# A token mixer in the frequency domain and a feed-forward layer in one kernel: uniform frequency slots, 96-row constants, part of batch 1 in the prologue, and a wider slot plan

## The chip, the cores and the metric

The kernel runs on one core of a Trainium2 chip. Its time is the device time of one execution in microseconds (us), as the median of several runs; smaller is better. The core's engines are TensorE (PE; its weight loads are shown as PEld), VectorE (DVE), ScalarE (ACT), GpSimd (POOL) and SyncE (SP, which only issues transfers here). Each works through its own instructions in the order in which they were written, and waits for the others by semaphores. POOL issues the transfers that change float32 into float16 on the way; SP issues plain ones.

## What is computed

```python
def _attn_ref(x, filt_r, filt_i):            # x: 8 batches x 3008 tokens x 256 channels
    X = np.fft.rfft(x, axis=1)
    F = (filt_r + 1j * filt_i)[None, :, :]   # 1505 frequencies x 256 channels
    return np.fft.irfft(X * F, n=x.shape[1], axis=1).astype(np.float32)

def _moe_ref(x, w_in, w_out):                # x: 24064 tokens x 256, d_ff = 2048
    h = x @ w_in
    g = np.maximum(0.01 * h, h)
    return (g @ w_out).astype(np.float32)
```

The first function mixes the 3008 tokens of a batch, channel by channel, by a filter on their Fourier transform; the second is applied to every token of the result. All inputs and the output are float32; the kernel computes in float16 with float32 sums.

## The kernel before

**The transform in two steps.** 3008 is 94 x 32, so the transform over the tokens is one over 94 (n1) and one over 32 (n2). For each batch the kernel runs this chain of stages:

- *s1* (16 groups, `s1_group`): two matmuls with the constants `f1_sb` (94 rows), 256 columns each, into one PSUM tile. ACT copies the tile to a buffer `big` as float16 (`spread`, L224).
- *t1* (4 parts, `t1_part`): DVE transposes blocks of 32 x 32 from one `big` buffer to the next (`turn`, L230).
- *s2* (12 groups, `s2_group`): one matmul with `small_sb` (L248; two in group 0, L246), then three products with the filter's real part `fa_sb` and imaginary part `fb_sb` on DVE (L252, L253, L254) and one sum on POOL (L256). Batch 0 uses another form, `s2_wide`: four columns at a time, two products on DVE (L272, L273), no POOL.
- *sa* (12 groups, `sa_group`, L284): the inverse over n2, copied to a third `big` buffer by ACT through `spread` (L224).
- *t2* (4 parts): transposes as in t1.
- *sb* (16 groups, `sb_group`, L300): four small matmuls with the constants `i1_sb`, copied by DVE (in batch 0 by DVE and ACT in turn) to `yts[b % 2]`, the batch's mixed tokens with the channels on the partitions (L303).

**The feed-forward layer in slots.** The 24064 tokens are cut into 47 chunks of 512. A chunk takes eight slots of `moe1_group` (4 matmuls of 512 columns, L322, then the leaky ReLU on ACT, L327) and, one chunk later, eight slots of `moe2_slice` (8 matmuls of 256 columns, L335; every fourth slot ACT copies the sum out, L339, and SP stores it). So there are 376 slots, and eight at the end with the second product alone. The chunks of one batch are 47 slots long.

**What sets the order.** The order is written by hand, with no scheduler. Batch 0 runs all its stages before slot 0; this is the prologue. The stages of batch b from 1 on are handed to slots by `plan`, with a base of 0 for batch 1 and 47(b-1)-8 for the others, to be done when the chunks reach that batch. Within a slot PE gets `moe1_group`, then the stages' groups in the order in which `plan` put them there, then `moe2_slice`. As PE works in order, a group that waits holds up the second product of its own slot and all that follows.

**The buffers that tie the stages together.** s1, s2, sa and sb take their PSUM tiles from one pool, `pfp`, of two tiles, in turn: a group waits until the tile's last reader, two groups before, is done with it. `moe1_group` and `s2_wide` use the pool `php` (two tiles), `moe2_slice` the pool `pop` (two tiles). `x_sb` holds one batch's input, so the load of the next waits for the last s1 matmul. The three `big` buffers rotate from stage to stage.

**Special cases of the frequency layout.** The 94-point step keeps 47 frequencies k1 and packs the special one at 0 and that at 47 into one place. So group 0 of s2 and sa uses other matrices (`fwd2(1)`, `inv2(1)`), the filter needs extra one-row loads (L183, L200), memsets (L191, L192, L204, L205), and a copy and a sign change of the filter to the upper 64 partitions, which `filt_copy` makes on DVE (L186, L187). L206 clears a whole `big` buffer on DVE.

**Loads in the prologue.** SP issues `f1_sb` in two halves of 94 rows, `small_sb` and `i1_sb`. POOL issues x of batch 0 in eight pieces (L162), the filter in pieces of 16 rows (L176, L180, L183), `w_in`, `w_out`, and x of batch 1. From the ninth on, each of POOL's transfers waits for the one eight before it to land.

Of the kernel before, what the change touches and what calls it, by code (L numbers as in the profile page):

```python
# [22 lines left out]

def _build_np_constants(N):
    n1 = np.arange(N1)
    c = np.arange(NC)
    fwd1 = np.zeros((P, N2, P))
    inv1 = np.zeros((P, N2, N1))
    for n2 in range(N2):
        for s, (qr, qi) in enumerate(((0, 2), (1, 3))):  # L30
            k1 = c + NC * s
            ang = 2 * np.pi * (np.outer(n1, k1) / N1 + n2 * k1[None, :] / N)
            co, si = np.cos(ang), np.sin(ang)
            ire, iim = 2 * co, -2 * si
            re, im = co, -si
            if s == 0:
                alt = np.cos(np.pi * n1)
                re[:, 0], im[:, 0] = 1.0, alt
                ire[:, 0], iim[:, 0] = 1.0, alt
            else:  # L40
                for m in (re, im, ire, iim):
                    m[:, NC - 1] = 0.0
            fwd1[:N1, n2, qr * Q : qr * Q + NC] = re
            fwd1[:N1, n2, qi * Q : qi * Q + NC] = im
            inv1[qr * Q : qr * Q + NC, n2, :] = ire.T / N1
            inv1[qi * Q : qi * Q + NC, n2, :] = iim.T / N1
# [8 lines left out]
    r_0, i_0, r_47, i_47 = (np.zeros((N2, N2)) for _ in range(4))
    r_0[:, 0] = 1.0
    i_0[:, 0] = np.cos(np.pi * n2)
    j = np.arange(1, h)
    r_0[:, 1:h] = np.cos(2 * np.pi * np.outer(n2, j) / N2)
    i_0[:, 1:h] = -np.sin(2 * np.pi * np.outer(n2, j) / N2)  # L60
    j = np.arange(h)
    r_47[:, h:] = np.cos(2 * np.pi * np.outer(n2, 1 + 2 * j) / (2 * N2))
    i_47[:, h:] = -np.sin(2 * np.pi * np.outer(n2, 1 + 2 * j) / (2 * N2))


    sg = np.where(k2 < h, 1.0, -1.0)[None, :]
# [4 lines left out]
    fwd2 = np.zeros((P, 2, P))
    inv2 = np.zeros((P, 2, P))
    for sp in range(2):
        f, g = np.zeros((P, P)), np.zeros((P, P))
        for s in range(2):
            if sp and s == 0:
                blk(f, 0, 0, r_0), blk(f, 0, 2, i_0)
                blk(f, 2, 0, r_47), blk(f, 2, 2, i_47)
                w0 = np.full((N2, 1), 2.0)
                w0[0] = 1.0  # L80
                blk(g, 0, 0, w0 * r_0.T), blk(g, 2, 0, w0 * i_0.T)
                blk(g, 0, 2, 2 * r_47.T), blk(g, 2, 2, 2 * i_47.T)
                continue
            blk(f, s, s, co), blk(f, s + 2, s, si)
            blk(f, s, s + 2, -si * sg), blk(f, s + 2, s + 2, co * sg)
            blk(g, s, s, co.T), blk(g, s + 2, s, -(si * sg).T)
            blk(g, s, s + 2, si.T), blk(g, s + 2, s + 2, (co * sg).T)
        fwd2[:, sp, :] = f
        inv2[:, sp, :] = g / N2
# [8 lines left out]
def kernel(  # L98
# [35 lines left out]
    fny_sb = cpool.tile([1, D], FP16, name="fny_sb")  # L134
# [13 lines left out]
    def fwd2(sp):  # L148
        return small_sb[:, sp, :]

    def inv2(sp):
        return small_sb[:, 2 + sp, :]

    def inv2x(sp):
        return small_sb[:, 4 + sp, :]
# [16 lines left out]
    def filt_load(dst, src, c0, c1):  # L172
        h = N2 // 2
        for s in range(2):
            q = s * Q
            nc.gpsimd.dma_start(  # L176
                dst[q : q + h, c0:c1], rows(src, NC * s + c0, N1, 1, h, c1 - c0))

            lo, hi = max(c0, 1 - s), min(c1, NC - s)
            nc.gpsimd.dma_start(  # L180
                dst[q + h : q + Q, lo:hi], rows(src, N1 - NC * s - lo, N1, -1, h, hi - lo))
        if c0 == 0:
            nc.gpsimd.dma_start(dst[h:Q, 0:1], rows(src, N1 // 2, N1, 1, h, 1))  # L183

    def filt_copy(c0, c1):
# [1 line left out]
        nc.vector.tensor_scalar(out=fb_sb[64:P, c0:c1, :], in0=fb_sb[0:64, c0:c1, :],  # L187
                                scalar1=-1.0, scalar2=None, op0=AL.mult)
# [17 lines left out]
    nc.vector.memset(big[2][:], 0.0)  # L206
# [4 lines left out]
    def s1_group(b, g):  # L211
        def go():
            ps = pfp.tile([P, 2, D], FP32, tag="pf", name=f"s1_b{b}_g{g}")
            for j in range(2):
# [1 line left out]
                nc.tensor.matmul(ps[:, j, :], f1_sb[:, n2, :], x_sb[:N1, n2, :],  # L216
                                 start=True, stop=True)
            spread(big[(4 * b) % 3], g, ps)
# [3 lines left out]
    def spread(dst, g, ps):  # L222
        o = dst[:].rearrange("p (e n t) -> p e n t", n=Q, t=2)[:, :, ds(2 * g, 2), :]
        nc.scalar.copy(o, ps[:].rearrange("p n (e t) -> p e n t", t=2))  # L224

    def turn(src, dst, i, parts):
        w = D // 2 // parts
# [2 lines left out]
        nc.vector.transpose(o, a)  # L230
# [195 lines left out]
```

## Time and profile before

| | us |
|---|---|
| time, median of 3 runs (859.57 to 862.3) | 860.71 |
| the profiled execution's own time | 862.13 |
| its span, from the first to the last instruction | 860.4 |
| first matmul of the feed-forward layer starts at | 88.12 |
| PE busy, share of the span | 775.4, 90% |
| ACT busy | 547.6, 64% |
| DVE busy | 372.5, 43% |
| POOL busy | 130.4, 15% |

In the profile the numbers of tiles are left out, so `f1_sb` reads f_sb, `i1_sb` reads i_sb, the PSUM tiles of s1 and of s2 both read s_b_g (s_b_w for the wide form), those of sb sb_b_g and those of sa sa_b_g. A row of the timeline has the start, the length, the engine, the line, the operation, what is written and read, how many instructions were merged, and in brackets the engine's idle time before it with what ended that. A line number tells the stage, but L216 is every s1 matmul and L224 every copy by `spread`, whatever the batch.

### The profile page before, as it was taken

Reading aid. Unit: us, or ns where it says so; the run is one execution under the profiler, and the core shown is the slowest. Engines: PE = TensorE matmul, PEld = TensorE weight load, DVE = VectorE, ACT = ScalarE, POOL = GpSimd, SP = SyncE. Lnnn points to the kernel's source line nnn. Section 1 sums busy time; section 2 is a strip of 40 time slices with the busy share of each in tenths; the row PEclk is TensorE's granted clock in tenths of the full one; section 3 lists DMA queues with packets and bytes.
Section 4 is the critical chain, followed back from the end, with each engine's and each line's share of the span. In section 5 each row is a group of like instructions: output and inputs, shape, how many; then the busy total and the mean of one; then the engine's idle time right before and its main releaser. Section 6 shows DMA issues by size and latency. Waiting matters only on the chain.

```text
span 860.4 us, 13332 instructions
## 1 busy us (share of the span) xinstructions
PE 775.4 (90%) x5725; PEld 528.4 (61%) x5725; DVE 372.5 (43%) x458; ACT 547.6 (64%) x704; POOL 130.4 (15%) x131
## 2 busy tenths in 40 slices
PE   0334879999999999999999999999999999999998
PEld 0112445776567756776567856776577756776666
DVE  0197176607742377307651476307651476300000
ACT  1313846686666866586666866586667766566663
POOL 4300024002400042002400042002400042000000
PEclk9996899999999999999999999999999999999999
DMA  7670030004011410114110401114011101011111
GB/s 153 105 136 1 13 85 25 29 34 109 26 38 37 98 37 25 38 40 94 38 37 26 110 25 37 37 38 97 26 37 38 37 26 37 26 37 46 41 38 50
DMA packets 31803, 43.21 MB, mean 50 GB/s; under 512 B 2266, under 2 KB 30010, under 8 KB 31086
## 3 DMA queue, kind: packets, MB, share of 16 engines
q0 software_dynamic: 5696, 15.98, 10.4%
q1 hardware_dynamic: 26048, 26.38, 8.8%
q8 instruction: 45, 0.74, 0.4%
q14 instruction: 14, 0.11, 0.0%
HBM read 33.69 MB, written 24.64 MB: 68 GB/s over the span
## 4 chain that ended last, share of the span: by engine, by line
PE 72%; DVE 19%; DMA 4%; issue 2%; ACT 2%; POOL 1%; DVEq 0%; ACTq 0%; POOLq 0%
PE o_c_t L335 32%; PE h_c_g L322 31%; DVE p_b_g L253 5%; DVE p_b_g L252 5%; DVE p_b_g L254 4%; PE sb_b_g L300 3%; PE s_b_g L216 3%; DVE big L230 2%; PE s_b_g L248 2%; DMA fb_sb<-in_filt_i_dram 2%; DMA x_sb<-in_x_dram 2%; PE sa_b_g L284 1%; ACT big L224 1%; ACT gt_c L327 1%; DVE y_b_g L273 1%
## 5 line engine op out<-in xcount | busy, mean ns | idle before, releaser
L327 ACT ACTIVATE gt_c<-h_c_g 128x1024 f16<-128x1024 f32 x376 | 386.4, 1028 | 223.1 <-PE h_c_g L322 223.0
L335 PE MATMUL o_c_t<-w_out_sb,gt_c 128*128 128x256 f16 x3008 | 389.3, 273 | 0.0
L322 PE MATMUL h_c_g<-yt,w_in_sb 128*128 128x512 f16 (+7 forms) x1728 | 388.9, 353 | 0.3 <-DVE yt L303 0.3
L335 PEld LDWEIGHTS <-gt_c 128*128 128x128 f16 x3008 | 290.8, 98 | 107.3 <-issue 27.3
L322 PEld LDWEIGHTS <-w_in_sb 128*128 128x128 f16 x1728 | 163.5, 98 | 95.5 <-issue 2.1
L230 DVE STREAM_TRANSPOSE big<-big 128x1024 f32<-128x1024 f32 x64 | 116.2, 1929 | 192.2 <-ACT big L224 192.1
L256 POOL TENSOR_TENSOR y_b_g<-p_b_g,p_b_g 128x512 f16<-128x512 f32 x84 | 106.7, 1270 | 245.2 <-DVE p_b_g L254 242.4
L303 DVE CAST yt<-sb_b_g 128x376 f16<-128x376 f32 x120 | 60.7, 545 | 79.9 <-PE sb_b_g L300 79.9
L224 ACT CAST big<-s_b_g 128x512 f16<-128x512 f32 x128 | 69.9, 614 | 27.1 <-PE s_b_g L216 27.1
L252 DVE TENSOR_TENSOR p_b_g<-s_b_g,fa_sb 128x512 f32<-128x512 f32 x84 | 58.1, 692 | 60.0 <-PE s_b_g L248 47.5
L224 ACT CAST big<-sa_b_g 128x512 f16<-128x512 f32 x96 | 55.5, 581 | 27.6 <-PE sa_b_g L284 27.6
L216 PE MATMUL s_b_g<-x_sb,f_sb 94*128 94x256 f16 x256 | 44.1, 291 | 30.3 <-DMA f_sb<-fwd_const 27.4
L339 ACT COPY ost_c_t<-o_c_t 128x512 f32<-128x512 f32 x94 | 55.5, 591 | 18.3 <-PE o_c_t L335 13.7
L162 POOL DMA_DIRECT2D x_sb<-in_x_dram x22 | 11.8, 542 | 320.7 <-PE s_b_g L216 319.6
L253 DVE TENSOR_TENSOR p_b_g<-s_b_g,fb_sb 64x512 f32<-64x512 f32 x84 | 58.2, 693 | 1.1
L254 DVE TENSOR_TENSOR p_b_g<-s_b_g,fb_sb 64x512 f32<-64x512 f32 x84 | 57.4, 684 | 1.1
L216 PEld LDWEIGHTS <-f_sb 94*128 94x128 f16 x256 | 25.2, 102 | 46.4 <-DMA f_sb<-fwd_const 27.9
L300 PEld LDWEIGHTS <-big 128*128 128x128 f16 x512 | 30.8, 104 | 24.9 <-DVE big L230 8.6
L284 PE MATMUL sa_b_g<-y_b_g,small_sb 128*128 128x512 f16 (+1 forms) x117 | 41.4, 388 | 4.2 <-DVE y_b_g L273 2.7
L248 PE MATMUL s_b_g<-big,small_sb 128*128 128x512 f16 x77 | 29.1, 378 | 17.1 <-DVE p_b_g L254 15.7
L300 PE MATMUL sb_b_g<-i_sb,big 128*128 128x94 f16 x512 | 35.3, 215 | 9.9 <-DVE big L230 7.6
L284 PEld LDWEIGHTS <-small_sb 128*128 128x128 f16 x117 | 11.5, 102 | 21.4 <-issue 5.9
(33 smaller groups left out, 60.4 us busy)
## 6 DMA issues: line engine op xcount, KB each, us to landing
out_dram<-ost_c_t SPq DMA_DIRECT2D x94, 256.0 KB, 2.1
x_sb<-in_x_dram POOLq DMA_DIRECT2D x7, 1024.0 KB, 8.6
x_sb<-in_x_dram POOLq DMA_DIRECT2D x7, 480.0 KB, 10.5
x_sb<-in_x_dram POOLq DMA_DIRECT2D x4, 256.0 KB, 11.9
w_in_sb<-in_moe_w_in_dram POOLq DMA_DIRECT2D x1, 1024.0 KB, 8.4
w_out_sb<-in_moe_w_out_dram POOLq DMA_DIRECT2D x1, 1024.0 KB, 13.0
f_sb<-fwd_const SPq DMA_DIRECT2D x2, 376.0 KB
i_sb<-inv_const SPq DMA_DIRECT2D x1, 752.0 KB, 34.3
```

The costliest lines, as they stand in the source:

```text
L216: nc.tensor.matmul(ps[:, j, :], f1_sb[:, n2, :], x_sb[:N1, n2, :], start=True, stop=True)
L224: nc.scalar.copy(o, ps[:].rearrange("p n (e t) -> p e n t", t=2))
L230: nc.vector.transpose(o, a)
L252: nc.vector.tensor_tensor(p1[:], ps[:], fa, AL.mult)
L253: nc.vector.tensor_tensor(p2[0:64], ps[64:P], fb[64:P], AL.mult)
L254: nc.vector.tensor_tensor(p2[64:P], ps[0:64], fb[0:64], AL.mult)
L256: nc.gpsimd.tensor_tensor(y1[:], p1[:], p2[:], AL.add)
L284: nc.tensor.matmul(ps[:, ds(*js), :], m(sp), t[:, ds(*js), :], start=(i == 0), stop=(i == len(y) - 1))
L300: nc.tensor.matmul(ps[:, j, :], src[:, n2, ts(dt, P)], i1_sb[:, n2, :], start=True, stop=True)
L322: nc.tensor.matmul(ph[:, j, ds(o, ln)], w_in_sb[:, dt, ts(ct, P)], yts[b % 2][:, dt, ds(lo, ln)], start=(dt == 0), stop=(dt == NDT - 1),)
L327: nc.scalar.activation(gts[ci][:, ds(2 * g, 2), :], ph[:], AF.Lrelu)
L335: nc.tensor.matmul(po[:, tj % 2, :], gts[ci][:, ct, ts(tj, P)], w_out_sb[:, ct, :], start=(ct == 0), stop=(ct == NCT - 1))
```

## The change

- **Uniform slots for k1.** Frequencies 0 and 47 now have places of their own: 48 places, none special. Group 0 of s2 and sa has one form like the others, `small_sb` shrinks from 6 to 3 matrices, and the one-row loads, the small memsets and `fny_sb` are gone. The clearing of `big[2]` covers columns 24 to 31 alone and no longer stands behind anything on DVE.
- **Constants.** `f1_sb` has 96 rows (two are zeros; matmuls read 94) and comes in four parts. SP issues it and `small_sb` first. `i1_sb` is issued by ACT after the copies of s1.
- **The filter's upper half** is written by ACT (fa, L317 of the changed kernel) and by POOL (fb, L318) in place of DVE.
- **The prologue.** s1 of batch 0 takes tiles from two pools and is copied by ACT and DVE in turn. s1 of batch 1 is run between the sb groups of batch 0, with tiles from `pop` and copies by ACT. `sb_group` counts the lower 128 channels first, then the upper.
- **The slot plan.** For batches 2 to 7, with z = 47(b-1)-8: s1 in slots z-5 to z+2 (before z to z+7), t1 from z+4 (z+9), s2 from z+9 with 7 slots for 4 groups (z+13, 5 for 4), sa three slots after s2, t2 from z+34 (z+32), sb in z+39 to z+46 (z+36 to z+43). For batch 1: no s1, t1 from slot 0 (8), s2 from slot 4 with 6 slots for 4 groups (slot 11, one a slot), t2 from 26 (27), sb from 31 (30).

```diff
-    f1_sb = cpool.tile([N1, N2, P], FP16, name="f1_sb")
+    f1_sb = cpool.tile([R1, N2, P], FP16, name="f1_sb")      # R1 = 96
-    nc.sync.dma_start(f1_sb[:, 0:H2, :], f1_d.ap()[0])
+    for i in range(FP):                                      # FP = 4
+        nc.sync.dma_start(f1_sb[:, ts(i, step), :], f1_d.ap()[i])
+    nc.sync.dma_start(small_sb[:], small_d.ap())
     x_load(0, 4)
-    nc.sync.dma_start(f1_sb[:, H2:N2, :], f1_d.ap()[1])
-    nc.sync.dma_start(small_sb[:], small_d.ap())
-    nc.gpsimd.dma_start(fny_sb[:], filt_r[N // 2 : N // 2 + 1, :])
...
-    nc.vector.memset(big[2][:], 0.0)
     nc.gpsimd.dma_start(w_in_sb[:], moe_w_in.rearrange("(dt p) c -> p dt c", p=P))
-    nc.gpsimd.dma_start(w_out_sb[:], moe_w_out.rearrange("(ct p) d -> p ct d", p=P))
+    nc.vector.memset(big[2][:].rearrange("p (e n t) -> p e n t", n=Q, t=2)[:, :, NC:Q, :], 0.0)
...
-            spread(big[(4 * b) % 3], g, ps)
+            spread(big[(4 * b) % 3], g, ps, copy)
...
-            if g == 0:
-                for j in range(2):
-                    nc.tensor.matmul(ps[:, j, :], fwd2(1 - j), src[:, j, :], start=True, stop=True)
-            else:
-                nc.tensor.matmul(ps[:], fwd2(0), src[:, ds(2 * g, 2), :], start=True, stop=True)
+            s2_mm(b, 2 * g, ps[:])
...
-    def plan(b, base, t1, s2, t2, sb, step):
+    def plan(b, s1, t1, s2, step, lag, t2, sb):
         for g in range(16):
-            at(base + g // 2, s1_group(b, g))
+            if s1 is not None:
+                at(s1 + g // 2, s1_group(b, g))
+            at(sb + g // 2, sb_group(b, g, nc.vector.tensor_copy))
         if b + 1 < B:
-            at(base + 8, lambda: x_load(b + 1, 1))
+            at(0 if s1 is None else s1 + 8, lambda: x_load(b + 1, 1))
         for i in range(4):
-            at(base + t1 + i // 2, t1_part(b, i))
-            at(base + t2 + i // 2, t2_part(b, i))
+            at(t1 + i, t1_part(b, i))
+            at(t2 + i, t2_part(b, i))
         for g in range(12):
-            at(base + s2 + (step * g) // 4, s2_group(b, g))
-            at(base + s2 + 3 + (step * g) // 4, sa_group(b, g))
-        for g in range(16):
-            at(base + sb + g // 2, sb_group(b, g, nc.vector.tensor_copy))
+            at(s2 + (step * g) // 4, s2_group(b, g))
+            at(s2 + lag + (step * g) // 4, sa_group(b, g))
+    two = ((pfp, "pf"), (php, "ph"))
+    copies = (nc.scalar.copy, nc.vector.tensor_copy)
     for g in range(16):
-        s1_group(0, g)()
+        s1_group(0, g, two[(g // 2) % 2], copies[g % 2])()
+    nc.scalar.dma_start(i1_sb[:], i1_d.ap())
+    for c0 in (0, HC):
+        nc.scalar.copy(fa_sb[64:P, c0 : c0 + HC, :], fa_sb[0:64, c0 : c0 + HC, :])
+        nc.gpsimd.tensor_scalar(fb_sb[64:P, c0 : c0 + HC, :], fb_sb[0:64, c0 : c0 + HC, :],
+                                -1.0, None, AL.mult)
     x_load(1, 1)
-    filt_copy(0, HC)
+    nc.gpsimd.dma_start(w_out_sb[:], moe_w_out.rearrange("(ct p) d -> p ct d", p=P))
...
-    nc.sync.dma_start(i1_sb[:], i1_d.ap())
...
     for g in range(16):
-        sb_group(0, g, nc.scalar.copy if g % 2 else nc.vector.tensor_copy)()
-    plan(1, 0, 8, 11, 27, 30, 4)
+        sb_group(0, g, copies[(g + 1) % 2], two[(g // 2) % 2])()
+        s1_group(1, g, (pop, "po"))()
+    plan(1, None, 0, 4, 6, 3, 26, 31)
     for b in range(2, B):
-        plan(b, 47 * (b - 1) - 8, 9, 13, 32, 36, 5)
+        z = 47 * (b - 1) - 8
+        plan(b, z - 5, z + 4, z + 9, 7, 3, z + 34, z + 39)
```

**PE in a slot of the main loop.** Before, a slot held either sb groups of one batch or s1 groups of the next; this is the last sb slot of batch 1, in order, with what an instruction waits for in brackets:

```order
L322 MATMUL h_c_g_1193<-yt_70,w_in_sb 128x512
L300 LDWEIGHTS big_68
L300 MATMUL sb_b_g_1199<-i_sb,big_68 128x94 [waits DVE_49]
...
L300 MATMUL sb_b_g_1205<-i_sb,big_68 128x94 [waits DVE_49]
...
L335 LDWEIGHTS gt_c_902
L335 MATMUL o_c_t_1184<-w_out_sb,gt_c_902 128x256
```

In the changed kernel the last five sb slots of each batch hold the first five s1 slots of the next as well:

```order
L267 MATMUL h_c_g_1227<-yt_69,w_in_sb 128x512
L245 LDWEIGHTS big_67
L245 MATMUL sb_b_g_1233<-i_sb,big_67 128x94 [waits Activation_49]
...
L245 MATMUL sb_b_g_1239<-i_sb,big_67 128x94 [waits Activation_49]
...
L162 LDWEIGHTS f_sb
L162 MATMUL s_b_g_1245<-x_sb,f_sb 128x256 [waits DVE_49]
...
L162 MATMUL s_b_g_1249<-x_sb,f_sb 128x256 [waits DVE_49]
...
L280 LDWEIGHTS gt_c_896
```

Two s1 groups now stand between the sb groups and the second product, and each of them waits for DVE, the reader of the sb tiles of the same slot.

**POOL behind the filter loads.** Before:

```order
L180 DMA fb_sb<-in_filt_i_dram 16x11x256
L207 DMA w_in_sb<-in_moe_w_in_dram 128x2x2048
L208 DMA w_out_sb<-in_moe_w_out_dram 128x16x256
L162 DMA x_sb<-in_x_dram 64x8192
L162 DMA x_sb<-in_x_dram 30x8192
```

Now:

```order
L139 DMA fb_sb<-in_filt_i_dram 16x12x256
L152 DMA w_in_sb<-in_moe_w_in_dram 128x2x2048
L318 ISA
L318 TENSOR_SCALAR fb_sb<-fb_sb 64x3072 x2
L122 DMA x_sb<-in_x_dram 64x8192
L122 DMA x_sb<-in_x_dram 30x8192
L321 DMA w_out_sb<-in_moe_w_out_dram 128x16x256
```

The two sign changes of the filter moved from DVE to POOL, ahead of the load of batch 1's x, and `w_out` moved behind that load.

**ACT at the end of the prologue.** Now, from the last copy of sa on:

```order
L172 CAST big_68<-sa_b_g_287 128x2x128x2
L172 CAST big_67<-s_b_g_301 128x2x128x2
L248 CAST yt_69<-sb_b_g_305 128x94x4
L172 CAST big_67<-s_b_g_311 128x2x128x2
L172 CAST big_67<-s_b_g_321 128x2x128x2
L248 CAST yt_69<-sb_b_g_325 128x94x4
```

This pattern goes on for 16 s1 and 8 sb copies; before, only the 8 sb copies stood there.

More of the change, by code (lines that the diff above doesn't have):

```diff
@@ L21 @@
 Q = 32
+R1 = 96
+FP = 4
 def _build_np_constants(N):
[L25 to L39, printed above, removed]
-            else:
[L41 to L46, printed above, removed]
@@ L48, in _build_np_constants @@
-    n2 = np.arange(N2)
+    n1, n2 = np.arange(N1), np.arange(N2)
     h = N2 // 2
     k2 = np.concatenate([np.arange(h), np.arange(N2 - 1, h - 1, -1)])
+    sg = np.where(k2 < h, 1.0, -1.0)[None, :]
     th = 2 * np.pi * np.outer(n2, k2) / N2
     co, si = np.cos(th), np.sin(th)
[L55 to L66, printed above, removed]
+    fwd1 = np.zeros((R1, N2, P))
+    inv1 = np.zeros((P, N2, N1))
+    fwd2, inv2 = np.zeros((P, P)), np.zeros((P, P))
     def blk(m, qi, qo, v):
         m[qi * Q : qi * Q + Q, qo * Q : qo * Q + Q] = v
[L71 to L89, printed above, removed]
@@ L133 @@
     x_sb = cpool.tile([P, N2, D], FP16, name="x_sb")
-    fny_sb = cpool.tile([1, D], FP16, name="fny_sb")
     big = [cpool.tile([P, Q * D], FP16, name=f"big{i}") for i in range(3)]
@@ L146 @@
     ctx.enter_context(tc.manual_schedule())
[L148 to L155, printed above, removed]
+    fwd2, inv2, inv2x = (small_sb[:, i, :] for i in range(3))
     def x_load(b, parts):
@@ L219, in s1_group, with paired, spread, turn @@
         return go
[L222 to L227, printed above, removed]
+    def paired(t):
+        return t[:].rearrange("p (e n t) -> p n e t", n=Q, t=2)
+    def spread(dst, g, ps, copy):
+        copy(paired(dst)[:, ds(2 * g, 2)], ps[:].rearrange("p n (e t) -> p n e t", t=2))
+    def turn(src, dst, i, flat):
+        w = D // 2 // 4
@@ L372 @@
     for g in range(6):
-        if g == 1:
-            filt_copy(HC, NC)
         s2_wide(0, g)
```

93 lines of the change are left out of this document (47 added, 46 removed).

## The prediction

> **What bounds the kernel now.** I first cut the span into stages and read PE's busy time in each (columns: stretch, its length, then each engine's busy time with its instructions, granted clock, DMA share, GB/s).
>
> ```profile
> core 0: us, PE busy (x) PEld busy (x) DVE busy (x) ACT busy (x) POOL busy (x), PEclk, DMA share, GB/s
> 88.12:193.40 105.28, 97.12 (x681) 62.28 (x681) 47.40 (x60) 73.76 (x101) 16.54 (x15) 0.96 0.14 38
> 193.40:289.70 96.30, 94.10 (x717) 64.99 (x716) 47.47 (x60) 67.71 (x89) 16.35 (x15) 1.00 0.18 50
> ...
> 674.70:767.90 93.20, 90.99 (x689) 62.23 (x687) 47.45 (x60) 61.03 (x73) 15.23 (x12) 1.00 0.10 34
> 767.90:849.50 81.60, 81.60 (x593) 56.03 (x592) 0.00 (x0) 53.36 (x59) 0.00 (x0) 1.00 0.11 38
> ```
>
> The stretches are 47 slots each, cut where a slot's leaky ReLU ends. After the first, PE is the bound: idle for 2.2 us of 96.3, for none in the last. So there are three places for a gain: the 88.12 us ahead of slot 0, the 8.2 us of PE idle in the first 47 slots, and 2.2 us a batch. The waits of PE in 193.4 to 289.7 name the last of these (columns: us, times, longest):
>
> ```profile
> PE s_b_g L248 <- DVE p_b_g L254: 2.2, 5, 0.6
> ```
>
> The timeline shows what the prologue is made of:
>
> ```profile
> 1.23 4.27 POOL L162 DMA_DIRECT2D x_sb<-in_x_dram  x8 [0.78 <-POOLq L410]
> ...
> 19.87 1.03 PE L216 MATMUL s_b_g<-x_sb,f_sb 94*128 94x256 f16 x4 [19.87 <-DMA f_sb<-fwd_const]
> ...
> 20.82 0.57 POOL L180 DMA_DIRECT2D fb_sb<-in_filt_i_dram  x1 [0.41 <-DMA x_sb<-in_x_dram]
> ...
> 32.26 1.04 PE L216 MATMUL s_b_g<-x_sb,f_sb 94*128 94x256 f16 x4 [7.52 <-DMA f_sb<-fwd_const]
> ...
> 36.68 1.07 ACT L224 CAST big<-s_b_g 128x512 f16<-128x512 f32 x2 [0.19 <-PE s_b_g L216]
> ...
> 40.55 3.47 DVE L206 MEMSET big<- 128x4096 uint32 x1 [0.90 <-DMA fb_sb<-in_filt_i_dram]
> ...
> 46.52 7.08 DVE L230 STREAM_TRANSPOSE big<-big 128x1024 f32<-128x1024 f32 x4
> ...
> 54.70 1.23 DVE L272 TENSOR_TENSOR y_b_g<-s_b_w,fa_sb 128x1024 f16<-128x1024 f32 x1 [1.10 <-PE s_b_w L268]
> ...
> 72.13 7.08 DVE L230 STREAM_TRANSPOSE big<-big 128x1024 f32<-128x1024 f32 x4 [1.57 <-ACT big L224]
> ...
> 75.83 0.26 PE L300 MATMUL sb_b_g<-i_sb,big 128*128 128x94 f16 x1 [4.41 <-DVE big L230]
> ...
> 79.27 0.73 PE L300 MATMUL sb_b_g<-i_sb,big 128*128 128x94 f16 x7 [3.18 <-DVE big L230]
> ...
> 87.83 0.47 ACT L303 CAST yt<-sb_b_g 128x376 f16<-128x376 f32 x1 [0.64 <-PE sb_b_g L300]
> 88.12 1.87 PE L322 MATMUL h_c_g<-yt,w_in_sb 128*128 128x512 f16 x4 [0.33 <-DVE yt L303]
> ```
>
> PE waits for the halves of f1 until 19.87 and 32.26. x has landed by 20.82: POOL's ninth and later transfers each wait for an x piece, this one for the eighth. The filter lands last, and DVE's clearing and copies stand behind it. So t1 starts at 46.52, 9 us after s1 is done.
>
> **The start of the prologue after the change.** Other loads give the rates (KB each, median us to landing):
>
> ```profile
> x_sb<-in_x_dram POOLq DMA_DIRECT2D x7, 480.0 KB, 10.5
> ...
> w_in_sb<-in_moe_w_in_dram POOLq DMA_DIRECT2D x1, 1024.0 KB, 8.4
> ```
>
> f1's second half took 12.4 us more for 376 KB (32.26 less 19.87), 30 GB/s, where w_in moves 1024 KB in 8.4 us, so it used few of the engines, and x, on the same ones, was held too. If 96 rows spread over all, x alone needs 1.23 + 10.5 = 11.7 us; f1's 768 KB beside it cost at most 6 us at w_in's rate, and I take 3, as SP starts before POOL's first piece. x lands at 15 (bounds 12 and, as now, 20.8). The Trainium skill, page "DMA: Bandwidth & Descriptors", section "Why a DMA increments its semaphore by 16 and not by 1", says that a transfer runs on the largest number of engines up to 16 that divides its outer sizes: 2 for 94 rows, 16 for 96. The 30 GB/s agree; without the rule f1 stays late, which is the second rival below.
>
> The last s1 groups take 1.8 us (two copies of about 0.6 on each of two engines, and the first matmuls): s1 done at 16.8. The clearing (3.47) runs at the start. t1 takes 7.1: done at 23.9. The filter, 16 pieces with x's bytes, needs 10 us behind x plus 1 for i1: its first half is there at about 20.5, its last at 26.
>
> The sign change on POOL is not in the trace. Its nearest rows:
>
> ```profile
> L256 POOL TENSOR_TENSOR y_b_g<-p_b_g,p_b_g 128x512 f16<-128x512 f32 x84 | 106.7, 1270 | 245.2 <-DVE p_b_g L254 242.4
> ...
> L187 DVE TENSOR_SCALAR fb_sb<-fb_sb 64x3072 f16<-64x3072 f16 x2 | 1.9, 948 | 0.0
> ...
> L327 ACT ACTIVATE gt_c<-h_c_g 128x1024 f16<-128x1024 f32 x376 | 386.4, 1028 | 223.1 <-PE h_c_g L322 223.0
> ```
>
> From 0.95 us (the same operation on DVE) to 7.6 (3072/512 x 1.27). By bytes a partition, 12288 against 5120, POOL's own row gives 3.05; I take 4. The Trainium skill, page "GPSIMD Engine Reference", section "4.1 Engine selection", holds one-input work there to be about line-rate; an estimate from its 1.03 cycles an element at 1.2 GHz is 2.6 us, and the sum would be 1.4 us lower. No row here shows it.
>
> POOL is free at 21.5, so the first copy ends at 25.5, the second at 29.5; fa's copies on ACT (about 3 us each at L327's 1 ns an element) lie beside it. DVE's first product can start at 24.3, its second, which needs fb, at 25.5: where 54.70 stood before. From there to t2 it took 17.4 us, of which 1.9 were the filter's second pair of copies (0.95 each), now gone: t2 starts at 24.3 + 15.5 = 39.8 and ends at 46.9. x of batch 1, issued by POOL at 29.5 behind the copies, lands 10.5 us later, at 40, hidden by 7 us; with 7.6-us copies it would land at 48.
>
> **The end of the prologue.** sb before: 79.27 to 88.12. That its lower half comes first gains nothing: the second weight load waited for all four transposes (75.83, then 79.27), and the order still shows that wait. ACT now has 15 s1 copies (0.535 each, 1.07 for two) and 8 sb copies (0.47) ahead of slot 0: 11.8 us, plus 0.9 for the first matmuls and about 1.3 as PE's work per pair at half clock is as long as ACT's. So 14 us: slot 0 at 61 instead of 88.1, **-27**. Bounds: 57.5 with the early ends (x at 12, POOL at 0.95), 71 with the late ones.
>
> **The first 47 slots.** These rows price a slot:
>
> ```profile
> 175.12 1.04 PE L335 MATMUL o_c_t<-w_out_sb,gt_c 128*128 128x256 f16 x8
> ...
> 175.99 1.03 PE L322 MATMUL h_c_g<-yt,w_in_sb 128*128 128x512 f16 x4
> ...
> 176.86 0.60 PE L216 MATMUL s_b_g<-x_sb,f_sb 94*128 94x256 f16 x4
> ...
> 177.29 1.04 PE L335 MATMUL o_c_t<-w_out_sb,gt_c 128*128 128x256 f16 x8
> ...
> 207.00 0.38 PE L248 MATMUL s_b_g<-big,small_sb 128*128 128x512 f16 x1
> 207.22 1.04 PE L335 MATMUL o_c_t<-w_out_sb,gt_c 128*128 128x256 f16 x8
> ...
> 263.74 0.51 PE L300 MATMUL sb_b_g<-i_sb,big 128*128 128x94 f16 x8
> 264.09 1.03 PE L335 MATMUL o_c_t<-w_out_sb,gt_c 128*128 128x256 f16 x8
> ```
>
> From start to start: bare slot 1.74, s1 pair 0.43, s2 or sa 0.22, sb pair 0.35. Slots 0 to 7 have no second product. With s1 they ran at ACT's pace, 1.90 (1.02 for the ReLU, two copies). Now the transposes of batch 1 set it: they start 0.6 after slot 0 and end at 7.8, and PE reaches s2 in slot 4 before that. Three s2 groups in turn then cost DVE 2.1 each; sa 0 follows the second, and slot 8 ends at about 16. The other 38 slots: 66.3 bare, 10.2 for 8 s2, 10 sa, 8 sb pairs and 8 s1 pairs, 1.8 for four s2 waits of 0.45. Sum 94.3 without the overlap below, against 105.3: **-11**, give or take 3.
>
> **s2 of batches 2 to 7.** Where s2 waits, the chain of waits shows its matmuls 2.63 apart, with DVE's three products between:
>
> ```profile
> 125.09 0.39 PE s_b_g L248
> ...
> 127.72 0.39 PE s_b_g L248
> ```
>
> The five waits of 0.44 a batch come where s2 stands in adjacent slots: s2 and sa take the two tiles in turn, an s2 tile is free only after those 2.63, and a slot with both lasts 2.18. With 7 slots for 4 groups two such places are left (slots 7-8 and 14-15 of the phase; 0-1 use different tiles). Six batches at 1.3: **-8**.
>
> **The overlap of sb and s1: a new wait.** sb of batch b-1 fills slots z-8 to z-1, s1 of batch b z-5 to z+2: five slots hold both, for b = 2 to 7. Each takes sb, sb, s1, s1 from the two tiles of `pfp`, so the first s1 waits for DVE's copy of the first sb, the second for that of the second:
>
> ```profile
> 160.53 0.51 PE L300 MATMUL sb_b_g<-i_sb,big 128*128 128x94 f16 x8
> ...
> 160.91 1.01 DVE L303 CAST yt<-sb_b_g 128x376 f16<-128x376 f32 x2 [1.08 <-PE sb_b_g L300]
> ...
> 79.72 0.55 DVE L303 CAST yt<-sb_b_g 128x376 f16<-128x376 f32 x1 [0.51 <-PE sb_b_g L300]
> ...
> 80.33 0.78 PE L300 MATMUL sb_b_g<-i_sb,big 128*128 128x94 f16 x8 [0.33 <-DVE yt L303]
> ```
>
> From the start of sb: DVE starts at 0.38 and frees the tiles at 0.89 and 1.39; PE follows 0.06 later. So s1 runs at 0.95 and 1.45 and ends at 1.67, where the work alone is 0.35 + 0.43 = 0.78. That is 0.89 lost in a slot, and `moe2_slice` stands behind it on PE; nothing covers it. 30 slots: **+27** (bounds 0 and, were s1's ACT copy in the loop too, 1.3 a slot, 39).
>
> The merged group 0 saves two matmul starts a batch, hidden in the slot: 0. The three-matrix `small_sb` and the new order within the copies (same elements): 0, bounds within 1 us.
>
> **Sum.** -27 - 11 - 8 + 27 = -19 on the profiled execution's 862.1 (span 860.4, 1.7 around it); that is 1.4 above the median, so I forecast 860.7 - 19 = 842.
>
> **The rivals.** *The overlap costs nothing* (8%): 842 - 27 = 815. PE is in order and the order shows both waits, so I see little for it. *f1 stays on few engines* (6%): its last part lands at 32 as now, s1 ends at 34, t1 at 41, everything 17 us later: 859, no change. *The prologue's late ends* (17%): slow POOL copies or loads, slot 0 at 66 to 71: 847 to 852. *Slower: the granted clock falls in the overlapped slots* (5%). It halves after idle stretches:
>
> ```profile
> 72.00:80.00 8.00, 0.99 (x8) 0.71 (x9) 7.36 (x5) 0.10 (x1) 0.00 (x0) 0.51 0.00 0
> ...
> 65.30:72.10 6.80, 4.29 (x17) 1.19 (x14) 5.26 (x5) 3.81 (x7) 0.00 (x0) 1.00 0.00 0
> ```
>
> At half clock a slot's 2.5 us of matmuls take 5.0: 30 slots, +75, 917; eight such slots use up the gain of 19. Against it: at 63% busy, in pieces, the clock stayed 1.00 (second row), and an overlapped slot is 74% busy. The forecast itself has 62%, with 833 to 851 as its own range; 2% remain for a prologue earlier still.
>
> **How the numbers follow.** The range, 824 to 857, leaves out the first rival, the fourth and most of the second. Faster by more than 0.3% (2.6 us, about what can be told from no change): all but the second and fourth rivals, 0.90; within it 0.05; slower 0.05.
>
> **What would show it.** Right: f1's last wait gone by 18 us, DVE's first product at about 24, slot 0 near 61; two s2 waits a batch; and a new row in PE's waits, s1 for the DVE copy of sb, of some 27 us in 60 waits. Wrong: x landing past 20, POOL's sign change past 8 us, no such row, or a clock below 1.00 after slot 20.

## The result

| | before | after |
|---|---|---|
| median (us), and the runs' spread | 861.11 (859.57 to 862.3) | 839.62 (838.17 to 840.22) |
| profiled execution: time, span | 862.13, 860.4 | 840.22, 838.1 |
| slot 0's matmuls start at | 88.12 | 63.06 |
| PE busy, share of the span | 775.4, 90% | 775.2, 92% |
| ACT, DVE, POOL busy | 547.6, 372.5, 130.4 | 555.8, 371.3, 144.8 |

The ratio is 0.9749 (95% interval 0.9729 to 0.9769): faster by 21.5 us, where 842 had been forecast from 860.7. PE's busy time is the same to 0.2 us, so by these totals the gain is idle time of PE that went away. That the totals agree so well is chance: with most of the overlapped slots parted, PE's busy time is 767.4 (the run with s1 ten slots earlier, below), so some 8 us of waiting count as busy here. The times of before differ a little between the tables here (861.11 beside these runs, 860.12 and 862.41 beside the experiments), so experiments are compared by their ratio to the runs of before on the same chip.

**The stages.** The windows of the changed kernel, cut as the prediction cut those of before, where the leaky ReLU of a row's last slot ends (a row is 47 slots; columns as there: stretch, length, then each engine's busy time):

```profile
core 0: us, PE busy (x) PEld busy (x) DVE busy (x) ACT busy (x) POOL busy (x), PEclk, DMA share, GB/s
63.71:162.80 99.09, 90.06 (x650) 57.72 (x650) 54.70 (x64) 68.64 (x86) 17.18 (x16) 1.00 0.23 53
162.80:261.20 98.40, 95.07 (x714) 64.94 (x713) 47.46 (x60) 68.61 (x87) 16.28 (x14) 1.00 0.18 48
655.10:745.80 90.70, 90.09 (x683) 61.55 (x682) 40.17 (x56) 60.39 (x71) 15.25 (x12) 1.00 0.10 35
```

The second stretch is longer than before (98.4 where 96.3 stood) and PE idles for 3.3 us in it, not 2.2: the body of the kernel has become slower. The rows 1 to 5 end at 261.2, 359.7, 458.1, 556.6 and 655.1. Set against before, with what the terms of the prediction make of each stage:

| stage | before | after | difference | predicted |
|---|---|---|---|---|
| ahead of slot 0 (to 63.71, where PE runs on) | 88.12 | 63.71 | -24.4 | -27 |
| row 0 | 105.28 | 99.09 | -6.2 | -11 + 5 x 0.89 = -6.5 |
| rows 1 to 5 | 481.3 | 492.3 | +11.0 | 5 x (0.89 x 5 - 1.3) = +15.7 |
| row 6, with no overlap of sb and s1 | 93.2 | 90.7 | -2.5 | -1.3 |
| row 7 and the end | 92.5 | 92.3 | -0.2 | 0 |
| span | 860.4 | 838.1 | -22.3 | -19 |

**The waits.** PE's waits of the changed kernel (us in all, times, longest):

```profile
PE s_b_g L162 <- DVE yt L248: 14.0, 30, 0.5
...
PE s_b_g L195 <- DVE p_b_g L207: 6.2, 18, 0.9
```

The first row is new: s1 waits for DVE's copy of sb, once in each of the 30 slots that hold both. The second is s2's, 15.7 us in 38 waits before.

**An overlapped slot**, in the timeline of the changed kernel (start, length, engine, line):

```profile
140.30 1.03 PE L267 MATMUL h_c_g<-yt,w_in_sb 128*128 128x512 f16 x4
141.17 0.51 PE L245 MATMUL sb_b_g<-i_sb,big 128*128 128x94 f16 x8
141.54 1.01 DVE L248 CAST yt<-sb_b_g 128x376 f16<-128x376 f32 x2 [2.38 <-PE sb_b_g L245]
142.15 0.83 PE L162 MATMUL s_b_g<-x_sb,f_sb 94*128 94x256 f16 x4 [0.47 <-DVE yt L248]
...
142.82 1.04 PE L280 MATMUL o_c_t<-w_out_sb,gt_c 128*128 128x256 f16 x8
143.69 1.03 PE L267 MATMUL h_c_g<-yt,w_in_sb 128*128 128x512 f16 x4
```

From sb's start the first s1 follows by 0.98 and `moe2_slice` by 1.65 (predicted 0.95 and 1.67). The slot is 143.69 - 140.30 = 3.39 long, where its work alone is 1.74 + 0.35 + 0.43 = 2.52. The row of waits shows 14.0 us, half of the 26 that the slots lose (30 x 0.87). In each slot 0.47 us counts as idle. Another 0.16 is booked to the sb matmuls, which show 0.51 where s1 could have followed after 0.35. The last 0.24 lies within the merged row of four s1 matmuls: `moe2_slice` starts 0.67 after it, where two s1 groups add 0.43, and the wait for the second tile falls there.

**The prologue** of the changed kernel, in the order of time:

```profile
15.03 0.49 POOL L136 DMA_DIRECT2D fb_sb<-in_filt_i_dram  x1 [1.05 <-DMA x_sb<-in_x_dram]
15.36 1.87 PE L162 MATMUL s_b_g<-x_sb,f_sb 94*128 94x256 f16 x8 [0.21 <-ACT big L172]
18.06 7.11 DVE L181 STREAM_TRANSPOSE big<-big 128x1024 f32<-128x1024 f32 x4
21.09 15.91 POOL L318 TENSOR_SCALAR fb_sb<-fb_sb 64x3072 f16<-64x3072 f16 x2 [0.15 <-issue]
26.42 1.23 DVE L220 TENSOR_TENSOR y_b_g<-s_b_w,fa_sb 128x1024 f16<-128x1024 f32 x1 [1.25 <-issue]
29.11 1.23 DVE L221 TENSOR_TENSOR y_b_g<-s_b_w,fb_sb 128x1024 f16<-128x1024 f32 x1 [1.46 <-POOL fb_sb L318]
36.96 1.15 POOL L122 DMA_DIRECT2D x_sb<-in_x_dram  x2
37.03 1.23 DVE L221 TENSOR_TENSOR y_b_g<-s_b_w,fb_sb 128x1024 f16<-128x1024 f32 x1 [0.48 <-POOL fb_sb L318]
44.93 7.09 DVE L181 STREAM_TRANSPOSE big<-big 128x1024 f32<-128x1024 f32 x4 [2.15 <-ACT big L172]
52.08 0.42 PE L245 MATMUL sb_b_g<-i_sb,big 128*128 128x94 f16 x3 [3.19 <-DVE big L181]
63.06 0.38 PE L267 MATMUL h_c_g<-yt,w_in_sb 128*128 128x512 f16 x1
63.71 1.67 PE L267 MATMUL h_c_g<-yt,w_in_sb 128*128 128x512 f16 x7 [0.27 <-ACT yt L248]
```

x has landed by 15.4, when PE goes on with the last quarter of s1 and waits for a copy of ACT, not for x (POOL's transfer at 15.03 waits for the last piece but one). t1 runs from 18.06, and nothing waits for f1. POOL's sign change is the surprise: two instructions take 15.91 us. DVE waits for the first of them at 29.11 and for the second at 37.03.

### The profile page after: what moved, and what is told of

It is laid out like the page before. It is cut to its first block, busy times and chain, and to the rows that moved or that the text cites. A ratio compares the mean times of both kernels' runs of the same rounds, so it can differ in the third digit from the quotient of the medians.

```text
span 838.1 us, 13296 instructions
## 1 busy us (share of the span) xinstructions
PE 775.2 (92%) x5708; PEld 525.8 (63%) x5708; DVE 371.3 (44%) x457; ACT 555.8 (66%) x698; POOL 144.8 (17%) x130
## 4 chain that ended last, share of the span: by engine, by line
PE 82%; DVE 10%; DMA 2%; POOL 2%; ACT 1%; issue 1%; DVEq 0%; POOLq 0%; ACTq 0%
PE o_c_t L280 38%; PE h_c_g L267 36%; DVE yt L248 3%; PE s_b_g L195 3%; PE s_b_g L162 2%; PE sa_b_g L230 2%; PE sb_b_g L245 2%; DVE big L181 2%; DVE p_b_g L207 2%; DVE p_b_g L206 2%; DVE p_b_g L205 2%; DMA x_sb<-in_x_dram 1%; ACT big L172 1%; DMA fb_sb<-in_filt_i_dram 1%; POOL fb_sb L318 1%
## 5 line engine op out<-in xcount | busy, mean ns | idle before, releaser
L172 ACT CAST big<-s_b_g 128x512 f16<-128x512 f32 x120 | 66.8, 611 | 23.6 <-PE s_b_g L162 22.3
L162 PE MATMUL s_b_g<-x_sb,f_sb 94*128 94x256 f16 x256 | 48.7, 296 | 27.5 <-DVE yt L248 14.0
L172 ACT CAST big<-sa_b_g 128x512 f16<-128x512 f32 x96 | 57.4, 601 | 9.1 <-PE sa_b_g L230 9.1
L122 POOL DMA_DIRECT2D x_sb<-in_x_dram x22 | 11.8, 541 | 246.2 <-PE s_b_g L162 245.4
L230 PE MATMUL sa_b_g<-y_b_g,small_sb 128*128 128x512 f16 x108 | 41.5, 409 | 6.2 <-DVE y_b_g L221 4.7
L195 PE MATMUL s_b_g<-big,small_sb 128*128 128x512 f16 x84 | 32.0, 381 | 7.9 <-DVE p_b_g L207 6.2
L195 PEld LDWEIGHTS <-small_sb 128*128 128x128 f16 x96 | 9.6, 101 | 33.5 <-DVE p_b_g L207 16.0
```

Of the source, the lines that this page charges most:

```text
L162: nc.tensor.matmul(ps[:, j, :], f1_sb[:N1, n2, :], x_sb[:N1, n2, :], start=True, stop=True)
L172: copy(paired(dst)[:, ds(2 * g, 2)], ps[:].rearrange("p n (e t) -> p n e t", t=2))
```

## The experiments

The theory after the result: the overlap of sb and s1 costs some 26 us through the two tiles of `pfp`; the 96 rows bring most of the prologue's gain; POOL's slow sign change costs a few us; s2's wider plan brings more than was forecast. The rivals: the overlapped slots are bound by something else (DVE's or ACT's work, and not the tiles); the gain ahead of slot 0 comes from the new order and not from the 96 rows; the sign change is covered. Each run alters the changed kernel in one respect; the last takes out the overlap and POOL's sign change together and spaces s2 wider, which no run does alone.

### The constants in 94 rows again

```diff
-R1 = 96
+R1 = 94
```

> The first-stage constants have 94 rows again, still in four parts and first in SP's queue; nothing else is changed. Theory (94 rows go over few DMA engines, about 30 GB/s): the last part of the 752 KB lands at about 25 to 32 us in place of under 8, x lands late with it, and slot 0 moves from 63.7 to 72 to 80: 848 to 856 us. Rival (the four parts and their place ahead of x made the difference): within 3 us of 839.6.

Measured: 858.34 us, ratio 0.9978 (0.9963 to 0.9992). That is beyond the 848 to 856 that the theory gave. The four parts are still there, and so is everything else of the change. f1's transfers in this run (KB each), and the timeline:

```profile
f_sb<-fwd_const SPq DMA_DIRECT2D x4, 188.0 KB
```

```profile
9.35 1.89 PE L162 MATMUL s_b_g<-x_sb,f_sb 94*128 94x256 f16 x8 [9.35 <-DMA f_sb<-fwd_const]
...
17.21 0.55 POOL L139 DMA_DIRECT2D fb_sb<-in_filt_i_dram  x1 [0.81 <-DMA x_sb<-in_x_dram]
...
20.77 1.89 PE L162 MATMUL s_b_g<-x_sb,f_sb 94*128 94x256 f16 x8 [9.54 <-DMA f_sb<-fwd_const]
...
28.40 1.89 PE L162 MATMUL s_b_g<-x_sb,f_sb 94*128 94x256 f16 x8 [5.74 <-DMA f_sb<-fwd_const]
35.84 1.89 PE L162 MATMUL s_b_g<-x_sb,f_sb 94*128 94x256 f16 x8 [5.56 <-DMA f_sb<-fwd_const]
38.57 7.14 DVE L181 STREAM_TRANSPOSE big<-big 128x1024 f32<-128x1024 f32 x4
...
62.63 7.08 DVE L181 STREAM_TRANSPOSE big<-big 128x1024 f32<-128x1024 f32 x4 [1.57 <-ACT big L172]
...
81.40 1.67 PE L267 MATMUL h_c_g<-yt,w_in_sb 128*128 128x512 f16 x7 [0.27 <-ACT yt L248]
```

s1 gets its second part of 188 KB 11.4 us after the first, while x is still landing, and the last two 7.5 us apart (25 GB/s), where the changed kernel's parts of 192 KB landed in 4.8 us (median), all four in flight together. Slot 0 comes at 81.40, 17.7 us later: two rows of zeros carry 17.7 of the 24.4 us ahead of slot 0 (19.7 by the ratios of all runs), and 94 rows leave the kernel 0.2% from before. This is the time that the prediction's second rival had (859). One part of the reasoning falls: x, which was to be held up with f1, had landed by 17.2, against 15.4. The Trainium skill, page "DMA: Bandwidth & Descriptors", section "Why a DMA increments its semaphore by 16 and not by 1", with its largest number of engines up to 16 that divides the outer size (2 for 94, 16 for 96), agrees with this pair of runs in the rates; no row here counts the engines.

The same rows show where the other 6.7 us come from. With f1 as late as before, t1 starts 8.0 us earlier than in the kernel before (38.57 against 46.52), as DVE's clearing and copies no longer stand ahead of it; from t1 to t2 it takes 1.6 less, and from t2 to slot 0 it takes 2.8 more, for s1 of batch 1. No run takes these edits apart, the uniform slots among them. In these two executions the 96 rows bring t1 forward by 20.5 us, not 17.7: some 2.8 are lost again on POOL's sign change, which in this run lies under the wait for f1 (t1 to t2 takes 24.1 here, 26.9 in the changed kernel).

### The sign change on DVE

```diff
-        nc.gpsimd.tensor_scalar(fb_sb[64:P, c0 : c0 + HC, :], fb_sb[0:64, c0 : c0 + HC, :],
-                                -1.0, None, AL.mult)
...
+    def flip(c0):
+        nc.vector.tensor_scalar(out=fb_sb[64:P, c0 : c0 + HC, :], in0=fb_sb[0:64, c0 : c0 + HC, :],
+                                scalar1=-1.0, scalar2=None, op0=AL.mult)
...
+    flip(0)
     for g in range(6):
+        if g == 2:
+            flip(HC)
         s2_wide(0, g)
```

> The sign change of the filter's imaginary part is made by DVE again (0.95 us each, the first behind t1, the second ahead of the third pair of products) in place of POOL (7.95 us each). Theory (POOL's two copies are what batch 0's products wait for, 1.5 and 0.5 us with the stalls that follow): the second transposes start at about 42.5 in place of 44.9, x of batch 1 is issued at 21 in place of 37; 837 us. Rival (the filter's landing at 28 holds the products anyway, and DVE pays 1.9 us for the copies): 839 to 841.

Measured: 836.98 us, ratio 0.9729 (0.971 to 0.9749). By ratios this is 1.7 us less than the changed kernel, with intervals that overlap, so the times alone do not settle it. The timeline of this run:

```profile
17.52 7.09 DVE L181 STREAM_TRANSPOSE big<-big 128x1024 f32<-128x1024 f32 x4
24.64 0.95 DVE L321 TENSOR_SCALAR fb_sb<-fb_sb 64x3072 f16<-64x3072 f16 x1
...
25.86 1.23 DVE L220 TENSOR_TENSOR y_b_g<-s_b_w,fa_sb 128x1024 f16<-128x1024 f32 x1 [0.27 <-issue]
27.01 1.21 DVE L221 TENSOR_TENSOR y_b_g<-s_b_w,fb_sb 128x1024 f16<-128x1024 f32 x1
...
30.51 0.95 DVE L321 TENSOR_SCALAR fb_sb<-fb_sb 64x3072 f16<-64x3072 f16 x1
...
42.22 7.08 DVE L181 STREAM_TRANSPOSE big<-big 128x1024 f32<-128x1024 f32 x4 [1.58 <-ACT big L172]
```

DVE does in 0.95 us what takes POOL 7.95. Its second product comes at 27.01 instead of 29.11, t2 starts 2.7 us earlier, slot 0 2.6 (61.14). Not all of that is the sign change: t1 began 0.5 earlier in this run, and the start of a profiled execution varies (slot 0 at 62.28 to 63.71 in the four with the changed kernel's whole prologue). From t1 to t2 the six runs with POOL's sign change and 96 rows take 26.3 to 27.7 us, this one 24.7. So POOL's sign change costs this kernel 1.6 to 3.0 us more than the same work on DVE, although DVE pays 1.9 us of its own time for it. x of batch 1 went out at 24.8 and not at 21, as POOL waited for the filter to land.

### s1 of the next batch ten slots earlier, clear of sb

```diff
-        plan(b, z - 5, z + 4, z + 9, 7, 3, z + 34, z + 39)
+        plan(b, z - 15, z + 4, z + 9, 7, 3, z + 34, z + 39)
```

> s1 of batches 2 to 7 starts 10 slots earlier (slot z-15 in place of z-5), where no sb stands; one slot in a batch (z-8) still holds both. Theory (the two-tile pool makes s1 wait for DVE's copy of sb, 0.86 us a slot): 24 of the 30 overlapped slots fall from 3.39 to 2.53 us, 839.6 - 21 = 819 us. Rival (the overlap is not what sets the length of these slots; PE would lose the time elsewhere): within 3 us of 839.6.

Measured: 819.59 us, ratio 0.9528 (0.9508 to 0.9548). PE's waits of this run have one overlapped slot a batch left:

```profile
PE s_b_g L162 <- DVE yt L248: 2.7, 6, 0.5
```

24 of the 30 overlapped slots are gone, and 19 us by ratios (0.0221 x 861); 24 x 0.87 is 21. Work and order of everything else are those of the changed kernel, but for the load of the next x, which goes out behind s1 and so ten slots earlier too. So the cost lies in the overlap; whether it is the tiles, this run alone does not say.

### s1 behind the second product of its slot

```diff
-                at(s1 + g // 2, s1_group(b, g))
+                late.setdefault(s1 + g // 2, []).append(s1_group(b, g))
...
         if ci > 0:
             moe2_slice(ci - 1, g)
+        for f in late.get(slot, ()):
+            f()
```

> The same slots hold sb and s1, but s1 stands behind the second product of its slot, so that DVE's copies of the sb tiles run under that product. Theory (only the place of the wait on PE matters): s1 would be due 1.2 us after sb began, its tile is free at 0.95; the wait is gone, about 839.6 - 25 = 815 us. Rival (a slot with both is long because DVE, ACT or PE have too much to do in it): unchanged, 837 to 842.

Measured: 817.77 us, ratio 0.9503 (0.9484 to 0.9522). The same slots hold sb and s1 as in the changed kernel, the same two tiles go round, and DVE and ACT have the same copies to make. Only what stands behind the wait on PE has changed (timeline):

```profile
138.69 0.60 PE L245 MATMUL sb_b_g<-i_sb,big 128*128 128x94 f16 x8
139.07 1.00 DVE L248 CAST yt<-sb_b_g 128x376 f16<-128x376 f32 x2 [1.80 <-PE sb_b_g L245]
139.13 1.03 PE L280 MATMUL o_c_t<-w_out_sb,gt_c 128*128 128x256 f16 x8
140.00 0.60 PE L162 MATMUL s_b_g<-x_sb,f_sb 94*128 94x256 f16 x4
140.44 1.03 PE L267 MATMUL h_c_g<-yt,w_in_sb 128*128 128x512 f16 x4
```

DVE's copies now run beside `moe2_slice`, s1 finds its tiles free, and the slot is 2.6 long (137.83 to 140.44, between the starts of the first product) instead of 3.39. The 30 slots of this kind take 2.52 to 2.93, 2.66 on average, which is 22 us less in all; by ratios the gain is 21 of the 26. The wait of s1 for DVE is gone from this run's list. That rules out DVE's and ACT's work as the bound: it was a wait for the tiles, in a place of PE's order where nothing covers it. (No run gives s1 tiles of its own in these slots.)

### The old slot plan for batches 2 to 7

```diff
-        plan(b, z - 5, z + 4, z + 9, 7, 3, z + 34, z + 39)
+        plan(b, z, z + 9, z + 13, 5, 3, z + 32, z + 36)
```

> The changed prologue and batch 1 as they are; batches 2 to 7 get the slots they had before (s1 from z, t1 z+9, s2 z+13 at 5 slots for 4 groups, t2 z+32, sb z+36). Theory (the new plan saves 1.3 us of s2 waits a batch and pays 4.3 for the overlap): 839.6 - 26 + 8 = 822 us; the new plan by itself is a loss of 18. Rival (the wider plan is worth its s2 waits and the overlap is paid elsewhere too): 839.6 + 8 = 848.

Measured: 826.61 us, ratio 0.9585 (0.9565 to 0.9604). So the new plan of batches 2 to 7, one part of the change, is a loss of 14 us by ratios; that is less than expected. Where the difference lies is seen in row 6, where no s1 overlaps. Windows of this run, and PE's waits in that row (638.6 to 731.9), then PE's waits in the changed kernel's row 6 (655.1 to 745.8):

```profile
156.70:253.00 96.30, 94.07 (x713) 64.36 (x712) 47.44 (x60) 67.99 (x88) 16.25 (x15) 1.00 0.18 50
638.60:731.90 93.30, 91.07 (x687) 61.75 (x686) 47.45 (x60) 61.32 (x74) 15.28 (x12) 1.00 0.10 33
```

```profile
PE s_b_g L195 <- DVE p_b_g L207: 2.2, 5, 0.7
```

```profile
PE s_b_g L195 <- DVE p_b_g L207: 0.6, 2, 0.3
```

Five waits became two, as predicted, and the idle time fell by 1.6 us. The row is 2.6 shorter (93.3 to 90.7). Some 0.5 of this is work that moved over the cut: in the old plan the last s1 pair of batch 7 falls behind the last leaky ReLU of row 5. The other 0.5 is what a wait costs beside its idle time, as PE's timeline of the old plan shows:

```profile
268.55 0.38 PE L230 MATMUL sa_b_g<-y_b_g,small_sb 128*128 128x512 f16 x1
269.58 0.39 PE L195 MATMUL s_b_g<-big,small_sb 128*128 128x512 f16 x1 [0.65 <-DVE p_b_g L207]
269.81 1.04 PE L280 MATMUL o_c_t<-w_out_sb,gt_c 128*128 128x256 f16 x8
...
273.50 0.38 PE L230 MATMUL sa_b_g<-y_b_g,small_sb 128*128 128x512 f16 x1
273.71 0.38 PE L195 MATMUL s_b_g<-big,small_sb 128*128 128x512 f16 x1
```

Without a wait s2 starts 0.21 after sa (the last two rows). The first s2 starts 1.03 after its sa, so some 0.8 is lost, but the row shows 0.65 as idle: the profile books sa with its whole 0.38, and only what lies behind that counts as a wait. So some 0.17 is lost beside each wait. The slots agree: those with waits of 0.31, 0.48 and 0.65 are 2.65, 2.83 and 2.99 long, where the work is 1.74 + 2 x 0.22 = 2.18. At three waits that makes 0.5. So the wider plan of s2 is worth 2.1 us a batch and not 1.3, and the overlap costs 0.87 x 5 = 4.35 of it back: 96.3 - 2.1 + 4.35 = 98.5, the length of rows 1 to 5 (98.4). Over six batches, 30 x 0.87 - 6 x 2.1 = 13.5, about the loss that this run gives back: 14 by ratios, 12.4 in the two profiled executions from slot 0 on (this one's slot 0 came 1.4 earlier, with the same prologue).

### s1 of batch 1 back in the slots

```diff
-        s1_group(1, g, (pop, "po"))()
...
-    plan(1, None, 0, 4, 6, 3, 26, 31)
+    plan(1, 0, 8, 11, 4, 3, 27, 31)
```

> s1 of batch 1 goes back from the prologue into slots 0 to 7, and batch 1's t1, s2 and t2 to the slots they had before; sb of batch 0 stands alone. Theory: slot 0 starts about 2.8 us earlier (52.0 + 8.9 in place of 63.7), but slots 0 to 46 take 10.5 us more, as before the change (105.3 with 4.3 of overlap, against 99.1): 839.6 + 7.7 = 847 us. Rival (ACT makes the same 16 copies in either place, so nothing is won by moving them): 837 to 842.

Measured: 842.73 us, ratio 0.9767 (0.9751 to 0.9784), 1.5 us more than the changed kernel by ratios, with overlapping intervals; the theory's 847 falls. The window of its row 0, which starts with the first product at 58.00:

```profile
58.00:166.10 108.10, 97.03 (x683) 61.22 (x683) 54.71 (x64) 75.62 (x101) 17.41 (x16) 0.98 0.21 49
```

Without s1 of batch 1 the prologue is 5.1 us shorter (58.00 against 63.06), and row 0 takes 8.4 longer (108.10 against 99.74 from the same start); t2 starts at the same time in both, to 0.02. By the profiles 3.4 us are won by the move, which is what the prediction's terms come to when they are put side by side: 11 in the slots less 15 copies x 0.535 = 8.0 on ACT ahead of slot 0, though each of the two came out some 3 us smaller. The timed runs cannot tell 3.4 from zero.

### The old order of channels in the prologue's sb

```diff
-        dt, h = g // 8, g % 8
+        dt, h = g % 2, g // 2
```

> sb takes the lower and the upper 128 channels in turn again, in all batches; nothing else is changed. Theory (the second weight load waits for all four transposes whatever the order): 839 to 840, no change. Rival (the lower half, done first, starts under the third and fourth transposes): 841 to 843, as the changed kernel would have gained 1 to 3 us by it.

Measured: 839.09 us, ratio 0.9729 (0.9714 to 0.9743): no difference from the changed kernel, as expected. The new order gains nothing because sb's second weights wait for all of t2 anyway (the row at 52.08 above).

### A plan without the overlap, one group at a time, and the sign change on DVE

```diff
-    plan(1, None, 0, 4, 6, 3, 26, 31)
+    plan(1, None, 0, 4, 6, 3, 26, 32)
...
-        plan(b, z - 5, z + 4, z + 9, 7, 3, z + 34, z + 39)
+        plan(b, z - 15, z + 1, z + 6, 8, 3, z + 32, z + 40)
```

and the sign change on DVE as above.

> All that the runs point to: s1 of batches 2 to 7 in slots z-15 to z-8 and sb one slot later (z+40; batch 1 from 32), so that no slot holds both; t1 from z+1, s2 from z+6 with 8 slots for 4 groups, so that no two s2 stand in adjacent slots; t2 from z+32; the sign change on DVE. Theory: 839.6 - 26 (overlap) - 6 (12 s2 waits of 0.48) - 2.5 (sign change) = 805 us. Rival (s2 waits and overlaps come back as others, since the stages are now closer to one another): 812 to 820.

Measured: 807.26 us, ratio 0.936 (0.9346 to 0.9374): faster than both kernels, by 55 and 33 us. s2 and sa now have a slot each, in turn, and s1 is done before sb begins. Windows of this run, row 1 and row 6:

```profile
156.00:249.50 93.50, 93.47 (x715) 64.92 (x714) 47.50 (x60) 68.42 (x87) 16.68 (x15) 1.00 0.19 51
623.10:712.60 89.50, 89.50 (x681) 61.60 (x679) 38.12 (x53) 59.89 (x71) 14.78 (x12) 1.00 0.10 35
```

PE idles for 0.03 us in row 1 and for at most 0.06 in each of the rows 2 to 6. From the prices of a slot, 47 x 1.74 + 24 x 0.22 + 8 x 0.35 + 8 x 0.43 = 93.3: rows 1 to 6 have nothing left but the matmuls. What is left of waiting lies ahead of slot 0 (60.31 us), in row 0 (95.69 us, with 89.08 of PE's work) and in the last 4 us or so.

## Why the prediction was right

Its time, 842, was 2.4 us above the measured 839.6, and its main mechanisms held: the 96 rows, the sb and s1 that meet, s2's waits. That it came so close is partly luck, as errors cancelled: of the span, the prologue came out 2.6 us longer than forecast and the rows from 1 on 6.1 shorter, and within the prologue 5 us too little ahead of t2 met 2.4 too much behind it.

- **f1 on all engines: right.** s1's wait for f1 is gone and x had landed by 15.4 (taken 15). With 94 rows the second rival came true to 1 us. That x had been held up by f1 was only partly so: 2 us in that run; what held x until 20.8 in the kernel before stays open.
- **The sign change on POOL: wrong size, by a factor of two.** Between the bounds 0.95 and 7.6 the prediction took 4, near the 3.05 of POOL's addition scaled by bytes. It took 7.95 for a half, just past the upper end; scaling by elements (2.48 ns each in the addition, 2.59 here) was the right reading. This, which cost 3.0 between the first product and t2 (18.5 against 15.5), and a later first product (26.42 against 24.3; s1 ended a good us late at 17.95, and s2's first matmuls and the start of the product took another) put t2 at 44.93, 5.1 after the 39.8 of the forecast. x of batch 1, issued behind the sign change at 36.96 and not at 29.5, was still hidden: s1 of batch 1 did not wait for it at 52. The Trainium skill, page "GPSIMD Engine Reference", section "4.1 Engine selection", would have it at about line-rate (the prediction's estimate from that page was 2.6 us); the run shows three times that, and the measurement decides.
- **The end of the prologue: wrong size the other way.** 14 us were allowed for sb of batch 0 with s1 of batch 1; it took 11.6 (52.08 to 63.71). ACT's first copy started 0.87 after sb, as the 0.9 for the first matmuls had it. From there ACT was busy for 10.72 of 10.76 us; so the copies took 1 less than the 11.8 that were counted, and the 1.3 for PE at half clock did not come on top. So -24.4 in place of -27.
- **Row 0: right** (-6.2 against -6.5; 38 bare slots are 66.1 us and not the 66.3 of the sum, which changes nothing). That batch 1's s1 makes this gain in the prologue at a price of 5 us there was in the terms, but under two headings; the net is about 3.
- **s2's two waits a batch: right in number, short in price.** A wait was priced at its idle time, 0.44. Without the 0.17 that the profile books to the matmul ahead of the wait, and with the two waits left at the size of the others (they are 0.31), the plan's gain was put at 1.3 a batch; it was 2.1, so about -13 instead of -8 over six batches.
- **The overlap: right.** 3.39 a slot against 1.74 + 1.67 = 3.41, 26 us against 27, for the reason given: the two runs that part s1 from sb, in slots or only in PE's order, give 19 and 21 us of it back. The row of waits has 30 entries and 14 us, not 60 and 27, for the reasons given at the overlapped slot.
- **The clock: the rival fell.** The slices of the changed kernel (tenths of the full clock) have the top digit from slot 0 on, and the windows above 1.00 in each row, the overlapped slots included:

```profile
PEclk9969999999999999999999999999999999999999
```

## What to carry to other kernels

A wait on an engine that works in order costs what stands behind it: before two stages are put into the same slot, follow the tiles that they take in turn, and if they must meet, put the waiting one behind the work that can cover it. A change that is faster as a whole can hold a step that loses: here edits worth some 35 us hid a new slot plan that cost 12 to 14, and the windows by stage, compared row by row, showed it at once. Where an operation moves to an engine that the trace shows only doing something else, the time per element of its nearest row was the better guide here than the time per byte; a run of that one operation settles it.

## What the runs showed of the hardware

- POOL took 7.96 us on average for a multiplication by a constant of 64 x 3072 float16 elements, 2.59 ns an element of a partition; its addition of two float32 operands, 128 x 512, takes 1.27 us, 2.48 ns an element. Neither the smaller type nor the single operand helped. Nor did an idle DVE: in the run with 94 rows the first half took just as long, with DVE busy for 1.4 us of it. DVE takes 0.95 for the same, a factor of 8 (groups of the changed kernel: instructions, busy time, mean ns of one):

```profile
L209 POOL TENSOR_TENSOR y_b_g<-p_b_g,p_b_g 128x512 f16<-128x512 f32 x84 | 106.7, 1270 | 302.1 <-DVE p_b_g L207 299.2 <-PE s_b_g L195 2.9
...
L318 POOL TENSOR_SCALAR fb_sb<-fb_sb 64x3072 f16<-64x3072 f16 x2 | 15.9, 7958 | 0.2 <-issue 0.2
```

- The same constants in 94 rows come at 25 GB/s in four parts (the last two 7.5 us apart) and at 30 GB/s in two halves; two rows of zeros take 17.7 us off the start.
- Where PE waits for a tile, more is lost than the profile shows as idle: waits of 0.31, 0.48 and 0.65 us made slots 0.47, 0.65 and 0.81 longer, since the matmul ahead is booked with 0.38 where the next can follow after 0.22.
